# Clustered attention and two gated layers on one core: a new written order of all operations, a third unpack buffer, pair passes in halves

## The chip, the cores and the metric

One core of a Trainium2 chip. The core has five engines that run their own instruction streams at once: TensorE (PE, matrix products and transposes; PEld is its weight load), VectorE (DVE), ScalarE (ACT), GpSimd (POOL), and SyncE (SP), which here issues every DMA. The metric is the device time of one execution in microseconds (us); lower is better.

## The reference

```python
# attention: q, k, v of shape (2, 8, 768, 64), 16 centroids for each of 8 heads
q_assign = argmax(q_n @ c_n.T); k_assign = argmax(k_n @ c_n.T)
mask = q_assign[:, :, :, None] == k_assign[:, :, None, :]
scores = where(mask, q @ k.T / 8, -1e9)
attn = softmax(scores)
x = (attn @ v), heads side by side          # (1536, 512)
# first layer, d_ff 1024
h = (x @ w1) * (x @ w2) @ w3;  x = h @ w_out   # (1536, 512)
# second layer, d_ff 2048
h = x @ w_in;  g = h * clip(h + 3, 0, 6) / 6
out = g @ w_out2                               # (1536, 512)
```

Everything is float32. Accuracy near float32 is kept by splitting an operand into a high and a low part in the `fp32r` format and adding three products (high-high, high-low, low-high).

## The kernel before, in words

The kernel is one flat list of about 4,000 operations (`op(key, engine, ...)`; `fop` is an operation that may run on one of several engines). Two tables written into the file fix everything about the order: `RANK` gives each operation its place in one common list, and `ON` gives a letter (a, d, p for ACT, DVE, POOL) to each operation with a choice. `Plan.order` sorts by `RANK`, and the instructions are emitted in that order. Each engine therefore works through its own operations in list order, and SP issues DMAs in list order; what an operation waits for is its data and a free buffer. `need` and the buffer counts of `Plan({...})` only constrain the list; the durations written beside each operation were for the search that found it.

The work runs in these stages. **Attention**, 16 heads of 768 rows in two halves (`hf`) and six row blocks (`c`): loads `lq`, `lk`, `lv`; transposes `T` on PE, their split `qkh` (ACT) and `qkl` (DVE); `pa`, the products with the centroids; `oh0` to `oh8`, nine small steps that turn them into one-hot codes; the moves `Dk`, `Ek`, `Dq`, `Ck`, `Cq` on SP; the scores `S1` and `S` (L745), the row maximum `mx` (DVE, L757), the exponential `ex` (ACT, L779); the transposes of the probabilities `pT` (L795) and their split into a high part `ph` (ACT) and a low part `pl` (DVE); the products with v, `av` (L819). With `WHOLE = 1`, head 0 alone is not split: its probabilities are copied whole (`p_all`), `pl` does not exist for it, and its `av` runs on plain float32 operands. After each pair of heads, POOL passes finish the pair on 128x768 tiles: `os` (L842, adds the two output parts), `pm` (L877, multiplies by the reciprocal denominators), and for the first four pairs `xh` and `xl` (the split of x for the next layer).

**Weights** are stored so that they have to be unpacked. For each of 72 blocks (`wo`, `w3`, `ab`, `set`): load `ld`, `c0` and `c2` on ACT (into the rings `cvt` and `cvs`), the clamp `c1` (L1002, DVE or POOL), `c3` and `c5` on DVE (L1011, L1015). A `cvs` buffer is free again when its block has been used; for an `ab` block that includes the store `abp` (L1127), which writes the block to DRAM, and for a `set` block the store `sst`. These blocks are interleaved with the attention.

**First layer**: w3 @ w_out is made during attention (`w`, L1062), `ab` (L1138) is x times w1 and w2 of the first four pairs, `x2` (L1253) the product with the combined matrix; the second batch half uses a seven-product scheme (`b`, L1390). **Second layer**: 16 steps `p` of seven products `h` (L1701) and output products `o` (L1745).

`idle` operations are matmuls on the identity whose result is not used; there are six groups of 2 to 5. `root` and `warm` are tiny ACT operations that call Sqrt and Exp; `cen2` (L527) also calls Sqrt.

```python
    def warm(func):
        if "warm" not in W_:
            W_["warm"] = at.tile([128, 1], F32, tag="warm", name="warm")
        nc.scalar.activation(out=W_["warm"], in_=three, func=func)
...
    op("root", "act", 0.2, lambda: warm(AF.Sqrt), due=-60)
    op("warm", "act", 1.4, lambda: warm(AF.Exp), ["cen2"], due=-5, after=[("qkh", 0, 1)])
    op("z", "act", 0.8, lambda: zero_rows(kk_[1]), due=61, after=[("qkh", 0, 1)])
```

Of the kernel before, what the change touches and what calls it, by code (L numbers as in the profile page):

```python
# [1852 lines left out]
```

## Time and profile before

| what | value |
|---|---|
| time, median of 3 runs | 756.61 us (754.64 to 757.69) |
| time of the profiled execution | 753.79 us |
| its span, first to last instruction | 751.9 us |
| first row maximum `mx` of head 0 / head 2 / head 9 / last | 19.8 / 60.4 / 200.7 / 352.5 us |
| first `x2` product in the long run of them, first `h` | 374.6 / 495.8 us |
| PE, DVE, ACT, POOL busy | 727.5, 621.8, 547.7, 196.0 us |

A busy share says how long an engine had an instruction in work, not how full it was: PE's instructions are pipelined. In a list of instructions, what stands in brackets is the idle time of the engine just before the instruction and the engine and tile that ended it. A line such as L426 or L423 is a helper's that many operations share; the tile's name tells which one it is (`cvs<-raw` is `c2`, `cvt<-raw` is `c0`, `pl<-ptr,ph` is `pl`).

### The profile page before, as it was taken

How to read it: one execution, taken by the hardware profiler on the slowest of the kernel's cores; microseconds unless marked ns; L12 is line 12 of the kernel's file. 1: busy time of each engine (PE TensorE's matmuls, PEld its weight loads, DVE VectorE, ACT ScalarE, POOL GpSimd, SP SyncE). 2: the span in 40 equal slices, each digit the busy share in tenths (PEclk: the TensorE clock that was granted, in tenths of full speed). 3: DMA queues.
4: the chain of work that ended last, by engine and by line, in shares of the span. 5: the costliest groups of instructions: out<-in, count | busy, mean ns of one | idle time of the engine just before them, and what ended most of it. 6: DMA issues, size and time to landing. Idle time of an engine off the chain costs nothing.

```text
span 751.9 us, 12041 instructions
## 1 busy us (share of the span) xinstructions
PE 727.5 (97%) x4143; PEld 661.9 (88%) x4143; DVE 621.8 (83%) x1076; ACT 547.7 (73%) x1040; POOL 196.0 (26%) x219
## 2 busy tenths in 40 slices
...
GB/s 217 198 141 174 157 128 201 127 136 125 197 109 159 160 132 178 108 141 86 161 195 224 223 129 112 177 214 128 158 123 70 45 68 130 81 71 80 46 29 85
DMA packets 81741, 101.97 MB, mean 136 GB/s; under 512 B 30960, under 2 KB 56592, under 8 KB 81680
## 3 DMA queue, kind: packets, MB, share of 16 engines
...
## 4 chain that ended last, share of the span: by engine, by line
PE 46%; DVE 4%; ACT 2%; issue 1%; POOL 0%; POOLq 0%; ACTq 0%; DVEq 0%
PE po L1745 16%; PE psh L1701 14%; PE psx L1253 8%; PE psab L1390 7%; PE psab L1138 1%; DVE gh L423 1%; DVE tt L1727 0%; PE av L819 0%; DVE m_gb L1608 0%; ACT tt L1723 0%; DVE m_sn L1715 0%; DVE m_gv L423 0%; ACT m_sn L426 0%; ACT m_whl L426 0%; PE ptr L795 0%
## 5 line engine op out<-in xcount | busy, mean ns | idle before, releaser
L757 DVE TENSOR_REDUCE den<-pst 128x1 f32<-128x768 f32 x96 | 91.2, 950 | 17.3 <-PE pst L745 14.8
L779 ACT ACTIVATE p<-pst,den 128x768 f32<-128x768 f32 x96 | 86.8, 904 | 14.5 <-DVE den L757 13.5
L423 DVE TENSOR_TENSOR pl<-ptr,ph 128x512 fp32r<-128x512 f32 x135 | 89.7, 680 | 7.7 <-ACT ph L426 7.4
L426 ACT ACTIVATE ph<-ptr 128x512 fp32r<-128x512 f32 x135 | 78.4, 596 | 16.1 <-PE ptr L795 14.6
L1138 PE MATMUL psab<-xT,abhl 128*128 128x384 f32 x384 | 81.1, 342 | 5.1 <-ACT asb L426 5.1
L1002 POOL TENSOR_SCALAR cvt<-cvt 128x512 f32<-128x512 f32 x43 | 40.9, 954 | 138.3 <-ACT cvt L426 113.3
L745 PE MATMUL pst<-kk,qkL 128*128 128x512 f32 (+1 forms) x192 | 71.6, 376 | 4.2 <-ACT p L779 3.8
L1138 PEld LDWEIGHTS psab<-xT,abhl 128*128 128x128 f32 x384 | 65.7, 188 | 7.2 <-ACT asb L426 5.8
L795 PEld LDWEIGHTS ptr<-id_r,praw 128*128 128x128 f32 x576 | 60.4, 140 | 7.4 <-ACT p L426 0.8
L819 PE MATMUL av<-ph,vs 128*128 128x384 f32 x180 | 63.3, 352 | 1.8 <-ACT T L426 1.8
L795 PE MATMUL ptr<-id_r,praw 128*128 128x128 f32 x576 | 64.4, 242 | 0.3 <-ACT p L426 0.2
L745 PE MATMUL pst<-kk,qkH 128*128 128x512 f32 (+1 forms) x192 | 64.2, 338 | 0.0
L426 ACT ACTIVATE m_sn<-psh 128x384 f32<-128x384 f32 x64 | 31.2, 488 | 44.2 <-PE psh L1701 43.7
L819 PE MATMUL av<-pl,vs 128*128 128x384 f32 x180 | 61.1, 339 | 0.0
L426 ACT ACTIVATE cvs<-raw 128x512 int32<-128x512 uint8 x72 | 47.9, 669 | 13.1 <-DMA abp<-cvs 7.3
L426 ACT ACTIVATE cvt<-raw 128x512 f32<-128x512 f32 x72 | 48.3, 672 | 11.1 <-DMA raw<-in_moe_w_out_dram 3.4
L1011 DVE SCALAR_TENSOR_TENSOR cvs<-cvt,cvs 128x512 int32<-128x512 int32 x72 | 52.5, 737 | 3.2 <-ACT cvs L426 2.3
L1062 PE MATMUL psw<-woh,wT 128*128 128x512 f32 x128 | 51.1, 414 | 0.0
L1015 DVE SCALAR_TENSOR_TENSOR cvs<-cvt,cvs 128x512 int32<-128x512 int32 x72 | 50.1, 699 | 0.3
L745 PEld LDWEIGHTS pst<-kk,qkL 128*128 128x128 f32 x192 | 36.0, 187 | 15.6 <-ACT p L779 12.6
L1723 ACT ACTIVATE tt<-m_sn,three 128x384 f32<-128x384 f32 x48 | 29.4, 613 | 19.5 <-DVE m_sn L1715 8.1
L1745 PE MATMUL po<-m_hl,m_gv 128*128 128x512 f32 x144 | 40.4, 393 | 0.0
...
## 6 DMA issues: line engine op xcount, KB each, us to landing
...
```

The lines of the kernel that those rows point to most:

```text
L423: nc.vector.tensor_tensor(out=out, in0=a, in1=b, op=ALU.subtract)
L426: nc.scalar.activation(out=out, in_=in_, func=AF.Copy, **kw)
L745: x = mm(out=psr[:, t, ks_], lhsT=TT[nm, h][:, i, cs_], rhs=flat(TT["K", h][:, a])[:, ks_], start=st, stop=sp)
L757: done["mx", n] = [other_banks(nc.vector.tensor_reduce(out=den_at(h, 0, c), in_=psS[h, c], axis=AX.X, op=ALU.max, negate=True), ("S", n + 1))]
L779: done["ex", n] = [other_banks(nc.scalar.activation(out=p, in_=psS.pop((h, c)), func=AF.Exp, bias=den_at(h, 0, c), accum_out=den_at(h, 1, ...
L795: x = nc.tensor.transpose(pt[:, blk(j)], raw[h, hf][0][:, c, blk(kb)], id_r)
L819: mm(out=t[:, 0:HF], lhsT=vs_t[h][:, 2 * s + i, :], rhs=x_[:, c0:c0 + HF], start=(s == 0 and i == 0 and n == 0), stop=(s == 2 and i == 1 a ...
L1138: mm(out=ps[:, 0:HF], lhsT=s[:, w, a, blk(kk)], rhs=xT0[0][:, x_, kk, hf * HF:hf * HF + HF], start=(kk == 0 and n == 0), stop=(kk == KD - ...
L1253: mm(out=ps[:, 0:HF], lhsT=Whl[0][:, a, j, blk(d)], rhs=gh[:, g_, j, :], start=(j == 0 and n == 0), stop=(j == J1 - 1 and n == 2))
L1390: mm(out=ps[:, 0:HF], lhsT=t[:, l, a, blk(kk)], rhs=bx[r][:, x_, kk, :], start=(st and kk == 0 and m == 0), stop=(kk == 1 and m == 2), ski ...
L1701: mm(out=ps[:, 0:HF], lhsT=left(p, l, a, kk), rhs=x[:, x_, kk, :], start=(st and kk == 0 and m == 0), stop=(kk == 1 and m == 2), skip_grou ...
L1745: mm(out=outs[b, c], lhsT=g[:, a, blk(c % 3)], rhs=w[:, w_, :], start=(first and a == 0 and w_ == 0), stop=(last and a == 1))
```

## The change

All of `RANK` is replaced, and twelve strings of `ON`. Beside the order, the code changes in five places: the ring `cvs` has three buffers in place of two; `os`, `pm` and `xl` are issued twice, on the 384 columns of each half, so that 19 POOL passes become 38, and `ab` products of a half need the `xl` of that half alone; `WHOLE` goes from 1 to 0, so head 0 is split as all others are; `cen2` may not come ahead of `root`; the first `ex` of a head may not come ahead of `warm`.

The two `RANK` tables can be compared between marks of the list. Operations of an engine that differ in number, before and after:

| list from / to | DVE | ACT | POOL |
|---|---|---|---|
| start / `S1` of head 0 | `c3` 2, 3; `oh0` 1, 2; `wtl` 1, 0; `Ck` 2, 1; `c1` 2, 1 | `root`, `warm`, `z`, `Ck` 0, 1 each; `c2` 2, 3; `wth` 2, 1 | `vlo` 1, 0; `oh1` 0, 1; `c1` 1, 2 |
| `S1` of head 0 / of head 2 | `pl` 3, 12; `wtl` 2, 3; `c3` 7, 6; `c1` 3, 2; `oh0` 2, 1; `oh1` 1, 0; `oh4` 1, 0 | `root` 1, 0; `z` 1, 0; `c0` and `c2` 7, 6; `ph` 12, 13 | `vlo` 1, 3; `vhi` 1, 2; `oh4` 1, 2 |
| `S1` of head 2 / of head 9 | `c1` 2, 4; `c3` 17, 16; `woh` 2, 1; `oh1` 1, 0; `oh4` 0, 1; `pw` 4, 5 | | `c1` 15, 13 |
| last `S` / first `x2` | `Wl` 1, 2; `pl` 6, 9; `c5` 2, 3; `c1` 1, 0 | | `Wl` 3, 2; `c1` 1, 2 |
| first `x2` / first `h` | `c1` 10, 18; `c3` 20, 23; `c5` 21, 23; `xwl` 6, 7; `Ll` 3, 4; `wol2` 3, 2 | `c0` 22, 24; `c2` 21, 23 | `c1` 10, 6 |

At the start, the DVE list before runs, from head 0's `oh0`: `oh0` to `oh4`, `c5`, `oh5`, `oh6`, `qkl` of head 1, `oh8`, another `qkl`, two `Ck`, `wtl`, `oh0` of head 1, `mx`. After: `oh0` to `oh4`, `qkl` of head 1, `oh5`, `oh6`, `c3`, `oh0` of head 1, `oh8`, one `Ck`, `c3`, `c5`, `c5`, `mx`; one `qkl` of head 1 stands ahead of `oh0`, and on PE half of head 1's transposes ahead of head 0's `pa`. The `idle` groups ahead of the first `S1` hold 11 matmuls before and 6 after; the first of them goes from place 5 to place 40.

```diff
@@ RANK
-    "root": "186",
-    "warm": "449",
-    "z": "105",
-    "idle": "5 79 97 112 45 37",
+    "root": "3",
+    "warm": "51",
+    "z": "43",
+    "idle": "40 62 135 151 81 100",
...
@@ ON
-    "Ck": "dd",
+    "Ck": "ad",
-    "pw": "pppdppppddapdpppaaapadddpdddddpp",
+    "pw": "ppppddppaaadaddpaaappappddapdpdd",
-    "oh1": "pddppppppddppdp",
+    "oh1": "pppppppppdpddpp",
-    "oh4": "pdppppppppdpppd",
+    "oh4": "ppdpppppppppppp",
-    "xh": "paaa",
+    "xh": "aaaa",
-    "woh": "adppddpp",
+    "woh": "appdaapd",
-    "Wl": "dppp",
+    "Wl": "pddp",
-    "Ll": "dddpdddpdddddddddddddddddpdddddd",
+    "Ll": "dddddddddddddddppddddddddddddddd",
-    "wol2": "ddddddddddddpdpdppdpppddpdpdddpd",
+    "wol2": "ddpddddddppdddddddddppddddddpdpp",
-    "xwl": "pddddddpdddddp",
+    "xwl": "dddddddddddddd",
-    "xs": "dddddddd",
+    "xs": "ddddddpd",
-    "c1": "ppddpdppddpdppppppppppppppdpdpppddpddpdpppppppdpdddpddppdppppppddddddddd",
+    "c1": "pppppdppdpdpdpppppddpppppdppdpdppppdppdpddddppddddppddppddddppddpdpdpddd",
...
-        "raw": 2, "rawx": 6, "cvt": 2, "cvs": 2, "hl": 2, "wT": 3, "m": 1, "s": 3, "r": 2, "a": 1, "x": 1, "x1b": 1,
+        "raw": 2, "rawx": 6, "cvt": 2, "cvs": 3, "hl": 2, "wT": 3, "m": 1, "s": 3, "r": 2, "a": 1, "x": 1, "x1b": 1,
...
-    op("cen2", "act", 0.2, cen_2, ("cen1",), due=-13.9)
+    op("cen2", "act", 0.2, cen_2, ("cen1", "root"), due=-13.9)
...
-    PHL, P32, WHOLE = [], [], 1
+    PHL, P32, WHOLE = [], [], 0
...
-    def o_sum(pr):
-        nc.gpsimd.tensor_tensor(out=Ts[pr], in0=Ts[pr], in1=W_["o"], op=ALU.add)
+    def o_sum(pr, hf):
+        nc.gpsimd.tensor_tensor(out=Ts[pr][:, hf], in0=Ts[pr][:, hf], in1=W_["o"][:, hf], op=ALU.add)
...
-    def pair_mul(pr):
-        T, rd = flat(Ts[pr]), flat(rdb.pop(pr))
-        if pr == KD:
+    def pair_mul(pr, hf):
+        r = slice(HF * hf, HF * hf + HF)
+        T, rd = flat(Ts[pr])[:, r], flat(rdb[pr])[:, r]
+        if pr == KD and hf == 0:
             xT1[0] = base.tile([128, KD, S], F32, tag="x1b", name="xT1")
-        out = T if pr < KD else xT1[0][:, pr - KD, :]
+        out = T if pr < KD else xT1[0][:, pr - KD, r]
         nc.gpsimd.tensor_tensor(out=out, in0=T, in1=rd, op=ALU.mult)
...
-    def pair_lo(e, pr):
-        sub_on(e, xT0[0][:, 1, pr, :], flat(Ts.pop(pr)), xT0[0][:, 0, pr, :])
+    def pair_lo(e, pr, hf):
+        r = slice(HF * hf, HF * hf + HF)
+        sub_on(e, xT0[0][:, 1, pr, r], flat(Ts[pr])[:, r], xT0[0][:, 0, pr, r])
...
-            op(("ex", h, c), "act", 0.88, lambda c=c: sexp(h, c), [("mx", h, c)] + [("ex", h, c - 1)] * (c > 0), due=t + 0.6, take=("p",),
+            op(("ex", h, c), "act", 0.88, lambda c=c: sexp(h, c), [("mx", h, c)] + ([("ex", h, c - 1)] if c else ["warm"]), due=t + 0.6, take=("p",),
...
-            nd = [("dB", h - 1), ("dB", h), ("oa", h, 0), ("oa", h, 1), ("oa", h - 1, 0), ("oa", h - 1, 1)]
             x = pr < KD
-            if oap(h):
-                op(("os", pr), "pool", 1.8, lambda: o_sum(pr), nd[2:], due=e + 3, drop=("O",))
-                nd = nd[:2] + [("os", pr)]
-            op(("pm", pr), "pool", 1.8, lambda: pair_mul(pr), nd, due=e + 4, drop=("rdb",) if x else ("rdb", "T"),
-               take=("x1b",) if pr == KD else ())
+            for hf in range(2):
+                nd = [("oa", h, hf), ("oa", h - 1, hf)]
+                if oap(h):
+                    op(("os", pr, hf), "pool", 0.93, lambda hf=hf: o_sum(pr, hf), nd + [("os", pr, 0)] * hf, due=e + 3 + 0.1 * hf, drop=("O",) * hf)
+                    nd = [("os", pr, hf)]
+                nd += [("dB", h - 1), ("dB", h)] + [("pm", pr, 0)] * hf + [("pm", KD, 0)] * (pr > KD)
+                op(("pm", pr, hf), "pool", 0.93, lambda hf=hf: pair_mul(pr, hf), nd, due=e + 4 + 0.1 * hf,
+                   drop=(("rdb",) if x else ("rdb", "T")) if hf else (), take=("x1b",) if pr == KD and hf == 0 else ())
             if x:
-                fop("xh", ("xh", pr), {"a": 0.75, "p": 0.9, "d": 0.5}, lambda e: pair_hi(e, pr), [("pm",
-                    pr)] + [("xh", 0)] * (pr > 0), due=e + 4.5, take=("x",) if pr == 0 else ())
-                fop("xl", ("xl", pr), {"p": 1.8, "d": 0.87}, lambda e: pair_lo(e, pr), (("xh", pr),), due=e + 4.6,
-                    drop=("T",))
+                fop("xh", ("xh", pr), {"a": 0.75, "p": 0.9, "d": 0.5}, lambda e: pair_hi(e, pr), [("pm", pr, 0), ("pm", pr, 1)]
+                    + [("xh", 0)] * (pr > 0), due=e + 4.5, take=("x",) if pr == 0 else ())
+                for hf in range(2):
+                    fop("xl", ("xl", pr, hf), {"p": 0.93, "d": 0.47}, lambda e, hf=hf: pair_lo(e, pr, hf),
+                        [("xh", pr)] + [("xl", pr, 0)] * hf, due=e + 4.6 + 0.1 * hf, drop=("T",) * hf)
...
-            s = cvo[key] = base.tile([128, 512], I32, tag="cvs", name="cvs", bufs=2)
+            s = cvo[key] = base.tile([128, 512], I32, tag="cvs", name="cvs", bufs=3)
...
-                       [("abl", j, w), ("xl", kk)] + ([("ab", j, hf, w, kk - 1)] if kk else []),
+                       [("abl", j, w), ("xl", kk, hf)] + ([("ab", j, hf, w, kk - 1)] if kk else []),
...
-        t = W_["osb", b, c] = base.tile([128, DM], F32, tag=("cvt", "cvs")[c % 2], name="osb", bufs=2)
+        t = W_["osb", b, c] = base.tile([128, DM], F32, tag=("cvt", "cvs")[c % 2], name="osb", bufs=(2, 3)[c % 2])
```

## Rows read from the trace of the kernel before

**Rows 1.** The profile's page: busy time, share of the span, instructions.

```profile
PE 727.5 (97%) x4143; PEld 661.9 (88%) x4143; DVE 621.8 (83%) x1076; ACT 547.7 (73%) x1040; POOL 196.0 (26%) x219
```

**Rows 2.** Windows: start:end, length, busy us of PE PEld DVE ACT POOL, granted clock.

```profile
0.00:19.80 19.80, 12.70 (x48) 9.59 (x49) 15.91 (x42) 9.81 (x17) 4.19 (x28) 1.00 0.79 217
19.80:60.40 40.60, 36.23 (x192) 26.81 (x191) 33.87 (x56) 37.06 (x69) 13.26 (x20) 1.00 0.59 159
104.40:142.50 38.10, 38.10 (x238) 32.70 (x237) 37.45 (x67) 34.58 (x70) 19.78 (x24) 1.00 0.55 146
352.50:374.60 22.10, 21.89 (x136) 20.81 (x133) 17.32 (x28) 18.11 (x31) 11.85 (x7) 1.00 0.40 135
374.60:495.80 121.20, 120.97 (x696) 120.65 (x697) 113.67 (x196) 80.45 (x142) 20.49 (x12) 1.00 0.55 179
```

**Rows 3.** Timeline, three stretches: ACT and PE.

```profile
209.03 0.66 ACT L426 ACTIVATE cvs<-raw 128x512 int32<-128x512 uint8 x1 [2.87 <-DMA abp<-cvs]
...
210.12 0.79 PE L1138 MATMUL psab<-xT,abhl 128*128 128x384 f32 x3 [2.85 <-ACT asb L426]
...
227.73 0.66 ACT L426 ACTIVATE cvs<-raw 128x512 int32<-128x512 uint8 x1 [1.83 <-DMA abp<-cvs]
...
229.45 0.44 PE L819 MATMUL av<-ph,vs 128*128 128x384 f32 x1 [1.63 <-ACT T L426]
...
301.17 0.66 ACT L426 ACTIVATE cvs<-raw 128x512 int32<-128x512 uint8 x1 [2.61 <-DMA abp<-cvs]
...
302.75 1.84 PE L1138 MATMUL psab<-xT,abhl 128*128 128x384 f32 x9 [2.11 <-ACT asb L426]
```

**Rows 4.** Timeline, 39.9 to 47 us: start, length, operation, idle before it.

```profile
39.95 1.28 ACT L505 ACT_TABLE_LOAD   x1
...
41.25 0.20 ACT L505 ACTIVATE warm<-three 128x1 f32<-128x1 f32 x1
...
43.51 1.28 ACT L779 ACT_TABLE_LOAD   x1
...
46.46 0.96 DVE L757 TENSOR_REDUCE den<-pst 128x1 f32<-128x768 f32 x1 [2.40 <-PE pst L745]
```

**Rows 5.** Timeline, transposes of head 1.

```profile
13.47 1.17 PE L607 MATMUL ptqk<-id_f,qkn 128*128 128x128 f32 x6
```

**Rows 6.** Groups by line: busy us, mean ns, idle before. Whole span.

```profile
L423 DVE TENSOR_TENSOR pl<-ptr,ph 128x512 fp32r<-128x512 f32 x135 | 89.7, 680 | 7.7 <-ACT ph L426 7.4
...
L420 POOL TENSOR_TENSOR vs<-vn,vs 128x384 fp32r<-128x384 f32 x15 | 15.3, 1018 | 0.6
...
L842 POOL TENSOR_TENSOR T<-T,O 128x768 f32<-128x768 f32 x7 | 13.4, 1915 | 12.9 <-ACT T L426 12.7 <-DMA qkH<-cd 0.2
...
L660 DVE STREAM_TRANSPOSE as<-pa 128x384 f32<-128x384 f32 x16 | 9.1, 569 | 0.1
...
L662 DVE TENSOR_TENSOR as<-as 128x192 f32<-128x192 f32 x6 | 2.7, 444 | 0.1
...
L668 DVE TENSOR_TENSOR as<-as,wtab 128x192 f32<-128x192 f32 x4 | 1.4, 358 | 0.1
```

**Rows 7.** Timeline around 38 us, POOL and DVE.

```profile
37.91 1.27 POOL L420 TENSOR_TENSOR wol<-cvs,woh 128x512 fp32r<-128x512 f32 x1
38.03 1.44 DVE L1002 TENSOR_SCALAR cvt<-cvt 128x512 f32<-128x512 f32 x1
```

**Rows 8.** The DMA stores of L1127 (abp).

```profile
DMA to landing us min/median/max: 2.0/2.7/4.1
```

**Rows 9.** Groups by line, DVE, 374.6 to 495.8 us.

```profile
L1015 DVE SCALAR_TENSOR_TENSOR cvs<-cvt,cvs 128x512 int32<-128x512 int32 x20 | 14.0, 700 | 0.1
...
L1011 DVE SCALAR_TENSOR_TENSOR cvs<-cvt,cvs 128x512 int32<-128x512 int32 x20 | 13.4, 685 | 0.6 <-POOL cvt L1002 0.5
...
L1002 DVE TENSOR_SCALAR cvt<-cvt 128x512 f32<-128x512 f32 x10 | 4.2, 418 | 0.0
...
L423 DVE TENSOR_TENSOR b_x<-xT,b_x 128x768 fp32r<-128x768 f32 x3 | 2.8, 947 | 0.0
```

More of the change, by code (lines that the diff above doesn't have):

```diff
@@ L61 @@
     "qkl": """
-        27 29 54 59 161 164 283 285 437 434 562 573 701 706 824 818 941 939 1056 1058 1184 1189 1307 1310 1453 1450 1576 1580 1700
-        1715 1860 1866""",
[3 rows of a table removed]
+        23 26 37 50 170 194 291 295 448 442 578 582 708 712 829 835 953 949 1082 1081 1199 1209 1331 1328 1459 1457 1591 1610 1736
+        1744 1871 1883""",
[3 rows of a table added]
     "Ck": """
-        67 62 139 136 253 249 370 383 532 525 646 659 786 795 903 898 1033 1035 1163 1155 1289 1271 1403 1408 1540 1536 1679 1673 1831
-        1823 1966 1950""",
+        70 69 155 140 269 252 417 405 542 548 671 668 795 791 923 929 1053 1048 1169 1178 1295 1291 1398 1411 1554 1556 1712 1702 1829
+        1833 1965 1969""",
@@ L106 @@
+        1967 2019 2073 2119""",
     "pT": """
[5 rows of a table removed]
-        2070 2086 2102 2114 2115 2134 2135""",
-    "ph": """
[5 rows of a table removed]
-        2073 2103 2108 2120 2124 2142 2144""",
[5 rows of a table added]
+        2101 2106 2122 2132 2144 2151 2171""",
+    "ph": """
[5 rows of a table added]
+        2111 2127 2133 2142 2155 2172 2174""",
+    "pl": """
[5 rows of a table added]
+        2116 2139 2143 2163 2167 2175 2177""",
     "av": """
[3 rows of a table removed]
-        1947 1980 1998 2017 2030 2049 2058 2089 2092 2118 2138 2149 2153""",
[3 rows of a table added]
+        1996 2028 2030 2048 2060 2089 2093 2117 2125 2147 2168 2178 2183""",
@@ new lines @@
+        2477 2770 2814 2680 3060 2492 2906 2978 3171 2721 2276 3108 2529 3190 2603 2802 2852""",
[5 rows of a table added]
+    "w": """
+        115 169 191 226 247 258 266 277 290 294 318 325 340 356 363 367 386 399 419 424 443 450 463 468 496 504 525 539 554 596 633
+        642 664 672 691 705 750 754 769 790 812 823 827 830 888 892 928 933 959 968 988 1009 1040 1045 1051 1080 1110 1127 1136 1151
+        1175 1180 1186 1191""",
[6 rows of a table added]
+    "ab": """
[5 rows of a table added]
+        2205 2209 2212""",
+    "aba": "1255 1330 1471 1412 1549 1599 1705 1767 1831 1882 1978 2021 1951 2169 2086 2200",
@@ L214 @@
+    "abg": "1283 1380 1502 1530 1646 1679 1733 1796 1854 1922 2001 2061 2146 2192 2123 2236",
+    "xdone": "2214",
+    "Wh": "2103 2120 2136 2158",
+    "Wl": "2110 2128 2149 2166",
+    "top": "2201",
+    "gsh": "2206 2210 2213 2219 2223 2234 2254 2295",
+    "gsl": "2211 2217 2221 2227 2231 2251 2279 2306",
+    "x2": """
[5 rows of a table added]
+        2911 2913 2915""",
[6 rows of a table added]
     "bsm": """
-        2225 2231 2290 2296 2316 2335 2364 2366 2381 2390 2396 2409 2420 2423 2426 2428 2461 2479 2490 2509 2531 2532 2535 2560 2568
@@ L236 @@
+    "bs": """
+        2347 2363 2369 2376 2408 2424 2434 2440 2463 2478 2484 2489 2521 2531 2538 2544 2574 2589 2597 2602 2620 2636 2641 2646 2665
+        2676 2682 2688 2704 2716 2722 2731""",
[8 rows of a table added]
     "sst": """
-        2491 2397 2297 2111 2121 2243 2328 2342 2236 2391 2200 2685 2595 2451 2162 2458 2794 2908 2842 3154 2635 3015 2836 3208 2747
-        2286 2954 2515 3211 2753 3056 3067""",
+        2546 2428 2302 2152 2097 2259 2358 2381 2247 2438 2207 2686 2559 2425 2185 2482 2831 2817 2684 3079 2496 2910 3029 3215 2725
+        2280 3113 2533 3225 2608 2805 2896""",
@@ L244 @@
-        3222 3223 3229 3289 3291 3292 3294 3340 3342 3344 3345 3392 3423 3432 3434 3495 3501 3502 3506 3565 3569 3586 3590 3633 3636
-        3639 3642 3703 3706 3708 3717 3766 3767 3770 3782 3835 3837 3838 3846""",
+        2819 2833 2843 2850 2892 2895 2898 2901 2951 2958 2965 2976 3024 3031 3035 3041 3106 3111 3114 3117 3160 3162 3164 3165 3248
+        3252 3255 3256 3298 3306 3310 3313 3367 3374 3380 3390 3439 3445 3454 3456 3506 3508 3510 3511 3561 3564 3566 3582 3643 3650
+        3657 3662 3710 3713 3727 3728 3785 3788 3789 3791 3845 3870 3871 3880""",
@@ L251 @@
-        3663 3730 3740 3795 3812 3871 3890""",
+        2861 2868 2909 2916 2985 2991 3049 3062 3127 3139 3199 3207 3265 3273 3325 3337 3397 3408 3462 3472 3530 3540 3601 3606 3681
+        3686 3745 3761 3800 3806 3896 3906""",
     "wf": """
-        2742 2752 2767 2840 2869 2914 2933 3054 3039 3167 3113 3220 3184 3264 3288 3382 3322 3418 3430 3474 3523 3522 3585 3637 3634
-        3746 3702 3775 3749 3796 3868 3870""",
+        2808 2838 2835 2894 2888 3026 3002 3104 3070 3184 3181 3249 3221 3311 3348 3414 3420 3478 3498 3520 3531 3614 3617 3676 3694
@@ L255 @@
+        3712 3738 3768 3838 3851 3909 3907""",
     "woh2": """
-        2757 2785 2801 2887 2902 3001 3007 3132 3074 3206 3163 3255 3263 3359 3311 3411 3381 3446 3476 3514 3577 3621 3602 3670 3697
-        3771 3731 3789 3791 3842 3927 3921""",
+        2822 2866 2878 2930 2928 3057 3030 3131 3175 3237 3209 3279 3272 3342 3388 3437 3465 3503 3512 3547 3585 3668 3640 3703 3718
+        3755 3777 3841 3852 3865 3927 3935""",
     "wol2": """
-        2763 2828 2863 2897 2926 3049 3020 3157 3093 3210 3177 3258 3283 3366 3314 3414 3426 3455 3493 3518 3581 3626 3631 3694 3699
@@ L282 @@
     "hr": """
[L283 to L285 removed]
+        2938 2952 2963 2966 2989 3010 3019 3022 3066 3080 3088 3094 3134 3151 3170 3172 3201 3228 3236 3244 3275 3293 3304 3309 3360
```

148 lines of the change are left out of this document (64 added, 84 removed), and 243 rows, old and new, of the table RANK.

## The prediction

> **What bounds the kernel now.** I read the page first. TensorE is busy 97% of the span, VectorE 83%, ScalarE 73%, GpSimd 26% [rows 1]. So nothing that shortens another engine's work counts unless TensorE was waiting for it, and there are only 751.9 - 727.5 = 24.4 us of such waiting. The table by stretch tells where it lies [rows 2]. The start (0 to 19.8 us) has PE idle for 7.1 us, the first two heads (19.8 to 60.4) for 4.4 us. From 104.4 to 142.5 PE is busy throughout, but so is VectorE, at 37.45 of 38.1 us, 98.3%: in the attention VectorE is close behind, and 98.3% is the fullest that I see it run. From 374.6 to 495.8, PE idles 0.2 us and VectorE 7.5 of 121.2 us. The granted clock is 1.00 in each stretch shown.
>
> The instructions in order of time then show where PE waits in the middle. Three times ScalarE's `c2` waits for the store `abp` that still reads the `cvs` buffer it wants: 2.87, 1.83 and 2.61 us, in all 7.3 us. Behind `c2` on ScalarE stand the copies that PE waits for (`asb`, or `T` from `av`), and PE stands idle 2.85, 1.63 and 2.11 us right after, in all 6.6 us [rows 3]. A second place is a pair of table loads: `root` loads Sqrt's table at 39.95 and `ex` loads Exp's again at 43.51, each 1.28 us on ScalarE; at 46.46 VectorE has stood 2.40 us waiting for scores [rows 4].
>
> **The change part by part.** The sum is made against the profiled execution's 753.8 us, which is 2.8 us below the median of 756.6; the same difference is then taken from the median.
>
> *Start.* Half of head 1's transposes come ahead of head 0's `pa`; that is half of an operation pair, and one of them took 1.17 us [rows 5]. On VectorE, between `oh0` and the first `mx`, one more `c3` and `c5` and `oh0` of head 1 (ahead of `oh8`) come in; one `Ck`, the `wtl` and one `qkl` leave. The chain pa, oh0 to oh8, Ck, S1, mx sets this stretch's end. If all that is put in falls into waits, it costs 0; if the transposes (1.17) and head 1's `oh0` (0.57, [rows 6]) lie on the chain, with a little of the unpacking, it costs 2. I take +1.0.
>
> *First two heads, 19.8 to 60.4.* Head 0 is now split. VectorE gets 9 more `pl`, and `wtl`, a subtraction of the same size (10 x 0.680 = 6.8), and loses `oh0`, `oh1`, `oh4` (0.569 + 0.444 + 0.358 = 1.4) [rows 6], one `c3` and one clamp (0.685 + 0.418 = 1.1, [rows 9]): +4.3, so 33.87 + 4.3 = 38.2 us. PE gets the split products in place of the plain float32 ones, which I count at nothing, because PE had 4.4 us to spare there [rows 2]. ScalarE is rid of both loads, 2.56 us [rows 4], and gets one `ph`. The two waits that come in (`cen2` for `root`, the first `ex` for `warm`) cost nothing: on ScalarE, which would hold up all that is queued behind them, both awaited operations stand earlier in its own order. So VectorE sets this stretch: at its fullest share, 38.2 / 0.983 = 38.8 us against 40.6, or -1.8. The bounds: all of the 2.40 us wait gone (-2.4); or VectorE fills no more of its time here than before (33.87 / 40.6 = 83%): the 4.3 less the 2.56 of the loads stay, +1.7.
>
> The Trainium skill, page "ScalarE: Activation LUTs", section "What ACT_TABLE_LOAD costs", counts a drain of some 1.38 us beside the load of 1.28. Here `warm` begins 0.02 us after its load's end [rows 4], so no drain shows behind the load; with it, the estimate by that page would free 5.3 us of ScalarE in place of 2.6, and the stretch would still be set by VectorE.
>
> *Port gaps.* A clamp on VectorE took 1.44 us under a GpSimd subtraction of 1.27 us [rows 7]; alone it takes 0.42 [rows 9], so one clash costs 1.0 us of VectorE. It matters only where VectorE sets the pace, that is from 60 to 200 us. I take 0.8 us there (below: nothing; above: 1.7, the price of a clash and two thirds of another). The halved passes stand beside this: a 128x384 subtraction took 1.018 us on GpSimd, and a 128x768 addition 1.915 [rows 6], so a pair of halves costs 0.1 us more than the whole, 2 us for 19 of them. GpSimd is idle three quarters of the span, which hides it, and without that cover 2 us is the cost; a half comes ready 0.9 us earlier.
>
> *Third `cvs` buffer.* The stores land 2.0 to 4.1 us after issue, 2.7 at the median [rows 8]. With a third buffer a `c2` takes a buffer whose store lies one block further back. I laid both lists out with the durations of the trace: for several `ab` blocks only 0.7 to 3.0 us of VectorE work lay between the store and the `c2` that takes its buffer before; afterwards it is 4.7 or more everywhere, which is beyond 4.1. So the 6.6 us of PE idle go. The other bound is 0. What the stall hid would be late next: `cvt` keeps two buffers, and `c0` stands in front of `c2`. I take -6.6, the value of [rows 3].
>
> *After the attention, 374.6 to 495.8.* Here the list brings VectorE 8 clamps that GpSimd did (8 x 0.418), 3 `c3` (0.685), 2 `c5` (0.700) and, net, one subtraction (`xwl` and `Ll` in, a `wol2` out; 0.947): 3.3 + 2.1 + 1.4 + 0.9 = +7.7 [rows 9]. That makes 113.67 + 7.7 = 121.4 us, as much as the whole stretch lasts. At 98.3% it lasts 123.5, so +2.3. If all of it fell into VectorE's 7.5 us of waits it would cost 0.2; if those waits stay, +7.7.
>
> The sum: +1.0 - 1.8 - 0.8 - 6.6 + 2.3 = -5.9. The profiled time becomes 747.9, the median 756.6 - 5.9 = **750.7 us**. What I have not named (heads 2 to 15, the second layer) is bound by PE with the same products and counts as zero.
>
> **The rivals.** What can be told from no change is 0.5%, 3.8 us: below 752.8 or above 760.4.
>
> *The wait moves on.* The third buffer frees ScalarE from waiting for the store, but `c2` then stands on data or on `cvt`, or the new order has its own late copy. For it: `cvt` and the raw buffers are as they were. Against: in the trace, each of the three stalls is put down to the store. Half of the 6.6 lost gives 754.0, all of it 757.3.
>
> *VectorE becomes the bound after the attention.* The 7.5 us that it idles from 374.6 to 495.8 are waits for PE's results that cannot be filled, so all of +7.7 stays; and from 352.5 to 374.6, where it has 4.8 us idle [rows 2], the list adds a `Wl` (two `pl`, 1.4), three `pl` (2.0) and a `c5` (0.7) less a clamp, 3.7. That gives 750.7 + 5.4 + 3.7 = 759.8, slower than before. It decides the sign once more than 5.9 us of these 9.1 are paid. For it: 98.3% was reached in one stretch only, and this one is the third as long as all attention. Against: VectorE has no long wait in it now.
>
> *PE's clock stays at its lower level (1.2 GHz) for part of the first two heads.* Before the first `S1` 6 unused products stand where 11 stood, and the first group comes at place 40 of the list, not 5. The column has 1.00 in the first 19.8 us [rows 2], with PE busy 64% of them, after those products. If a quarter of the next stretch's 36.2 us of PE work ran at half speed, 9.1 us more less the 4.4 idle give +4.7, 755.4; for half of it, +13.7, 764.4. It is slower than before by more than 0.5% from two fifths on. Against: the split products of head 0 give PE more work there. The Trainium skill, page "TensorE: Matmul & The Clock Gate", Part 1 on the clock gate, has the low level as the default and activity as what lifts it; no row here shows the low level.
>
> **How the numbers follow.** The forecast gets 0.60; the moved wait 0.20; VectorE late 0.13; the clock 0.07. The forecast's own range: everything at its better bound is -1.0 (start), -0.6, -0.9, -2.1, so 746.1; the worse bounds are not likely together, and the two largest (first heads +3.5, late +5.4, of which half each) give 755.2. For 8 in 10 over all cases I go a little below the better bound, for a gain that I did not find, and up to VectorE's case: 744.5 to 760.0. Faster by over 0.5%: 0.55 of the forecast's 0.60 and 0.03 of the moved wait, 0.58. Slower by over 0.5%: 0.09 from the VectorE case, with a bad start beside it, and 0.05 from the clock, 0.14. The rest, 0.28, is the same.
>
> **What the profile would show.** Right: no `cvs<-raw` with idle time put down to `abp`, and no PE idle of over 1.5 us behind an ACT `asb` or `T`; two table loads fewer; the first `mx` near 20.8 us, that of head 2 some 0.8 us earlier than now; the `x2`-to-`h` stretch near 123.5 us with VectorE at 98%. Wrong: a new wait of ScalarE on `cvt` or on raw data in the middle; VectorE below 94% and a longer stretch after 374.6; granted clock under 1.00 before 60 us. What would make the prediction wrong beyond that is an order that makes PE idle at many small places, which a sum of named terms cannot see.

## The result, and the profile after

The changed kernel took **747.21 us** at the median (746.43 to 748.33), against 756.15 us for the kernel before (754.64 to 757.69) in the same comparison: ratio 0.9883, 95% interval 0.9858 to 0.9907, 8.9 us less. The forecast was 750.7, in a range of 744.5 to 760.0; faster was right, and the size was forecast a third too small. The profiled execution took 746.43 us, its span 744.5. One execution among the experiments below, of e5, ran at a granted clock of 0.853 (787.66 us); it is left out of its ratio.

The page of the changed kernel, busy time of each engine (answers to [rows 1]):

```profile
PE 721.8 (97%) x4143; PEld 660.8 (89%) x4143; DVE 619.3 (83%) x1086; ACT 548.7 (74%) x1046; POOL 175.6 (24%) x229
```

The windows of the changed kernel between the same marks of the work: start, first `mx` of head 0, of head 2, of head 8, of head 14, first product of the long run of `x2`, first `h`, end. Columns as in [rows 2]; the last two are the DMA share and GB/s.

```profile
0.00:21.40 21.40, 9.46 (x39) 7.99 (x40) 14.96 (x41) 12.53 (x21) 5.33 (x29) 1.00 0.84 237
21.40:58.40 37.00, 34.32 (x210) 28.56 (x209) 36.14 (x63) 33.05 (x67) 17.24 (x24) 1.00 0.71 171
58.40:177.70 119.30, 118.47 (x748) 103.31 (x747) 115.46 (x201) 109.71 (x221) 51.16 (x67) 1.00 0.56 153
177.70:303.20 125.50, 125.14 (x823) 117.86 (x822) 113.86 (x193) 107.50 (x221) 54.03 (x67) 1.00 0.55 152
303.20:360.00 56.80, 56.22 (x362) 53.26 (x361) 46.75 (x77) 45.00 (x86) 24.28 (x23) 1.00 0.46 143
360.00:488.70 128.70, 126.92 (x723) 124.59 (x722) 124.04 (x216) 89.32 (x156) 6.47 (x8) 1.00 0.59 189
488.70:744.40 255.70, 251.23 (x1249) 225.27 (x1247) 168.08 (x304) 151.55 (x278) 17.07 (x12) 1.00 0.25 82
```

And the kernel before between the same marks, for the stretches that [rows 2] does not have:

```profile
60.40:180.30 119.90, 119.47 (x762) 104.48 (x761) 116.60 (x202) 107.52 (x217) 53.90 (x67) 1.00 0.56 151
180.30:314.10 133.80, 126.69 (x825) 118.72 (x824) 115.56 (x199) 107.84 (x219) 50.50 (x54) 1.00 0.58 155
314.10:369.70 55.60, 55.34 (x357) 52.33 (x356) 43.93 (x75) 44.52 (x85) 25.39 (x21) 1.00 0.40 120
369.70:495.70 126.00, 125.66 (x722) 124.66 (x721) 118.47 (x202) 85.25 (x150) 21.42 (x13) 1.00 0.55 177
```

(The long run of `x2` begins at 369.7 us there; the 374.6 of the small table and of [rows 2] lies 5 us inside it. The stretch is taken from its begin here.)

The reader sees where the 7.4 us between the two spans come from: start +1.6, heads 0 and 1 -3.6, heads 2 to 7 -0.6, **heads 8 to 13 -8.3**, last heads to `x2` +1.2, `x2` to `h` +2.7, the rest -0.4. In heads 8 to 13 PE stood idle 133.80 - 126.69 = 7.1 us before and 0.4 after; the other 1.6 us of the 8.3 are busy time of PE (126.69 to 125.14 us), and in the two stretches behind PE is busy 2.1 us longer than before. Outside heads 8 to 13 the whole new order comes out at +0.9.

The groups by line of the changed kernel show that the wait on the store is gone (the first line is the kernel before), that `cvt` waits no longer than the 11.1 us of before, and that the clamps on GpSimd have a mean of 700 ns (954 before):

```profile
L426 ACT ACTIVATE cvs<-raw 128x512 int32<-128x512 uint8 x72 | 47.9, 669 | 13.1 <-DMA abp<-cvs 7.3 <-DMA set<-cvs 5.7
...
L427 ACT ACTIVATE cvt<-raw 128x512 f32<-128x512 f32 x72 | 48.2, 671 | 9.1 <-DVE cvs L1021 4.6 <-DMA raw<-in_moe_w_in_dram 1.9 <-DMA raw<-in_moe_w_dram 1.7
L427 ACT ACTIVATE cvs<-raw 128x512 int32<-128x512 uint8 x72 | 48.1, 668 | 0.0
...
L1008 POOL TENSOR_SCALAR cvt<-cvt 128x512 f32<-128x512 f32 x40 | 27.9, 700 | 149.1 <-ACT cvt L427 125.4 <-DVE b_sn L1405 21.4 <-ACT praw L769 0.9
```

`c2` now waits for nothing, 0.0 us in 72, although the `abp` stores land later than before (median 4.8 us and at most 5.0 from issue to landing, against 2.7 and 4.1 in [rows 8]).

### The profile page after: what moved, and what is told of

It is laid out like the page before. It is cut to its first block, busy times and chain, and to the rows that moved or that the text cites. A ratio compares the mean times of both kernels' runs of the same rounds, so it can differ in the third digit from the quotient of the medians.

```text
span 744.5 us, 12074 instructions
## 1 busy us (share of the span) xinstructions
PE 721.8 (97%) x4143; PEld 660.8 (89%) x4143; DVE 619.3 (83%) x1086; ACT 548.7 (74%) x1046; POOL 175.6 (24%) x229
## 4 chain that ended last, share of the span: by engine, by line
PE 79%; DVE 9%; ACT 5%; DMA 4%; issue 2%; SPq 1%; POOL 0%; ACTq 0%; DVEq 0%; POOLq 0%
PE po L1751 17%; PE psh L1707 15%; PE pst L746 8%; PE av L820 8%; PE psab L1396 7%; PE psab L1144 7%; PE ptr L796 5%; PE psw L1068 5%; PE psx L1259 4%; DMA m_gb<-set 2%; PE pa L647 1%; DVE den L758 1%; ACT p L780 1%; PE ptqk L608 1%; DVE cvs L1017 1%
## 5 line engine op out<-in xcount | busy, mean ns | idle before, releaser
L424 DVE TENSOR_TENSOR pl<-ptr,ph 128x512 fp32r<-128x512 f32 x144 | 95.4, 679 | 6.8 <-ACT ph L427 6.1
L427 ACT ACTIVATE ph<-ptr 128x512 fp32r<-128x512 f32 x144 | 83.0, 594 | 10.5 <-PE ptr L796 8.2
L820 PE MATMUL av<-ph,vs 128*128 128x384 f32 x192 | 67.5, 352 | 0.0
L820 PE MATMUL av<-pl,vs 128*128 128x384 f32 x192 | 64.9, 338 | 0.3 <-DVE pl L424 0.3
L1008 POOL TENSOR_SCALAR cvt<-cvt 128x512 f32<-128x512 f32 x40 | 27.9, 700 | 149.1 <-ACT cvt L427 125.4
L427 ACT ACTIVATE m_sn<-psh 128x384 f32<-128x384 f32 x64 | 31.3, 489 | 32.0 <-PE psh L1707 31.3
L1017 DVE SCALAR_TENSOR_TENSOR cvs<-cvt,cvs 128x512 int32<-128x512 int32 x72 | 50.3, 702 | 1.4 <-issue 0.6
L1021 DVE SCALAR_TENSOR_TENSOR cvs<-cvt,cvs 128x512 int32<-128x512 int32 x72 | 49.5, 692 | 0.6
L1751 PE MATMUL po<-m_whl,m_gv 128*128 128x512 f32 x171 | 45.8, 392 | 0.0
```

The source lines that it names most:

```text
L424: nc.vector.tensor_tensor(out=out, in0=a, in1=b, op=ALU.subtract)
L427: nc.scalar.activation(out=out, in_=in_, func=AF.Copy, **kw)
L820: mm(out=t[:, 0:HF], lhsT=vs_t[h][:, 2 * s + i, :], rhs=x_[:, c0:c0 + HF], start=(s == 0 and i == 0 and n == 0), stop=(s == 2 and i == 1 a ...
L1017: stt(out=s, in0=cvt[key], scalar=3, in1=s, op0=ALU.logical_shift_left, op1=ALU.bitwise_or)
L1751: mm(out=outs[b, c], lhsT=g[:, a, blk(c % 3)], rhs=w[:, w_, :], start=(first and a == 0 and w_ == 0), stop=(last and a == 1))
```

## The experiments

In the edits, `MOVE` gives operations another place in the common list (35.3 is just behind place 35) and `ENG` another engine; all else stays. Every ratio is to the kernel before, on the same chip: e1 to e4, e5 to e8, e9 to e11 and e12 ran on four chips, and the median of before was 756.3, 756.8, 756.7 and 754.6 us there. Where two runs come from different chips, their ratios are the measure and the medians stand beside them.

| run | kernel | median us | ratio, 95% interval |
|---|---|---|---|
| e1 | before, `cvs` 3 | 747.78 | 0.9887 (0.9865 to 0.9908) |
| e2 | before, two table loads fewer | 753.58 | 0.9959 (0.9943 to 0.9975) |
| e3 | before, head 0 split | 759.80 | 1.0045 (1.0031 to 1.0060) |
| e4 | before, e1 + e2 + e3 | 749.03 | 0.9903 (0.9884 to 0.9923) |
| e5 | before, e1 + e2 | 744.81 | 0.9841 (0.9817 to 0.9865) |
| e6 | changed, head 0 unsplit | 749.89 | 0.9912 (0.9890 to 0.9934) |
| e7 | changed, transposes of head 1 put back | 747.47 | 0.9879 (0.9860 to 0.9899) |
| e8 | changed, 8 late clamps on GpSimd | 745.54 | 0.9854 (0.9833 to 0.9875) |
| e9 | e7, and the copies `cT` put back | 746.71 | 0.9869 (0.9849 to 0.9889) |
| e10 | e4, `pl` of head 0 later, 5 operations to GpSimd | 748.01 | 0.9897 (0.9876 to 0.9918) |
| e11 | changed, `os` and `pm` whole | 747.28 | 0.9878 (0.9859 to 0.9898) |
| e12 | e8 + e9, and PE's product `cT` put back | 744.26 | 0.9857 (0.9834 to 0.9879) |

**e1: the third buffer alone.**

```diff
-        "raw": 2, "rawx": 6, "cvt": 2, "cvs": 2, "hl": 2,
+        "raw": 2, "rawx": 6, "cvt": 2, "cvs": 3, "hl": 2,
...
-            s = cvo[key] = base.tile([128, 512], I32, tag="cvs", name="cvs", bufs=2)
+            s = cvo[key] = base.tile([128, 512], I32, tag="cvs", name="cvs", bufs=3)
...
```

> The kernel before, with a third cvs buffer and nothing else; its order is unchanged. Theory 1 (the store's wait is a matter of buffers): the three waits of ScalarE's cvs<-raw on the store (7.3 us) are gone, PE's 6.6 us of idle time behind them too, and the time falls by 6 to 7 us, ratio 0.991 to 0.992. Rival (the wait moves on): ScalarE reaches c2 earlier, but the old order lets it stand on cvt or on raw data instead; PE keeps half or more of the idle time, and the ratio is 0.996 to 1.000.

It gave 8.5 us, practically all that the whole change gave, in the order of before. The groups of ScalarE in e1:

```profile
L426 ACT ACTIVATE cvt<-raw 128x512 f32<-128x512 f32 x72 | 48.4, 672 | 14.1 <-DMA raw<-in_moe_w_in_dram 5.1 <-DMA raw<-in_moe_w_out_dram 3.5 <-DMA raw<-in_moe_w_dram 2.0
L426 ACT ACTIVATE cvs<-raw 128x512 int32<-128x512 uint8 x72 | 48.0, 671 | 0.1
```

`cvs` waits 0.1 us in place of 13.1, of which 5.7 were for the stores `set<-cvs` behind the attention; the stretches there are no shorter in e1 (from `x2` to `h` 126.5 us against 126.0, the rest 257.0 against 256.2). `cvt` waits 3 us longer over the span (11.1 before), but not where PE pays. Heads 8 to 13 in e1:

```profile
181.00:308.70 127.70, 126.63 (x827) 118.77 (x826) 116.76 (x200) 107.48 (x219) 50.47 (x54) 1.00 0.62 163
```

127.7 us against 133.8: 6.1 us, close to the 6.6 of [rows 3]. That the median fell by 2 us more is taken up with e2. The profiled execution of e1 is the slowest of its five: its granted clock fell at the first scores of head 0 (0.84 and 0.73), where no store is waited for, and the first `mx` of head 2 comes at 61.0 us against 60.4:

```profile
16.00:20.00 4.00, 2.75 (x12) 2.07 (x13) 3.89 (x8) 2.50 (x5) 1.84 (x4) 0.84 0.81 242
20.00:24.00 4.00, 3.63 (x15) 2.45 (x15) 3.84 (x8) 3.78 (x7) 1.61 (x3) 0.73 1.01 270
```

**e2: two table loads fewer.**

```diff
+MOVE = {"root": 2.5, "warm": 49.5}
```

> The kernel before, with root ahead of cen2 and warm ahead of head 0's first exponential, so that two of four table loads go (2.57 us of ScalarE). Theory 1 (the loads hold up the scores at 40 to 46 us): the first mx of head 2 comes 1 to 2.4 us earlier and the time falls by as much, ratio 0.997 to 0.999. Rival (VectorE or PE holds this stretch anyway): head 2 comes less than 0.5 us earlier, ratio 1.000.

The first `mx` of head 2 came at 57.8 in place of 60.4 (2.4 us of it in the stretch behind the first `mx`), and the median fell by 2.7 us: the first theory. But in e2's profiled execution the lead of 3.0 us at head 9 was 0.2 at head 10. The wait on the store lies there, and the windows and the instructions in order of time of e2 show what followed it:

```profile
200.00:204.00 4.00, 4.00 (x30) 3.80 (x30) 3.55 (x7) 3.14 (x7) 1.76 (x2) 1.00 1.02 260
204.00:208.00 4.00, 0.80 (x6) 0.66 (x5) 1.67 (x5) 1.62 (x4) 1.10 (x3) 0.78 0.12 46
208.00:212.00 4.00, 4.00 (x14) 3.81 (x13) 1.23 (x2) 2.00 (x5) 0.00 (x0) 0.50 0.42 131
212.00:216.00 4.00, 4.00 (x27) 3.77 (x27) 3.68 (x6) 2.26 (x5) 0.68 (x2) 0.86 0.04 8
216.00:220.00 4.00, 4.00 (x29) 3.83 (x29) 2.97 (x4) 3.50 (x8) 2.06 (x2) 1.00 0.75 182
```

```profile
206.38 0.66 ACT L432 ACTIVATE cvs<-raw 128x512 int32<-128x512 uint8 x1 [3.19 <-DMA abp<-cvs]
207.47 1.33 PE L1144 MATMUL psab<-xT,abhl 128*128 128x384 f32 x3 [3.20 <-ACT asb L432]
```

PE stood idle 3.20 us, and then had a granted clock of 0.50, its lower level of 1.2 GHz, from 208 to 212: 14 matmuls in 4 us where 29 and 30 ran in 4 us at 1.00. From the first `mx` of head 9 to that of head 10 e2 needs 25.3 us, the profiled execution of before 22.5, where the same wait (2.85 us, [rows 3]) was followed by a clock of 1.00. First e2, then before:

```profile
197.70:223.00 25.30, 22.10 (x130) 20.66 (x129) 17.90 (x31) 17.64 (x38) 8.03 (x9) 0.87 0.48 124
200.70:223.20 22.50, 19.64 (x129) 18.24 (x128) 17.87 (x32) 17.64 (x38) 8.01 (x9) 1.00 0.53 137
```

For the same products PE was busy 22.10 us in place of 19.64. So a store's wait costs its own length, and in e2 it cost 2.5 us more in clock. In e3, which has two buffers too, the clock fell behind another of the three waits, one of 2.15 us, and not behind those of 2.03 and 2.08:

```profile
308.00:312.00 4.00, 4.00 (x16) 4.00 (x15) 2.06 (x5) 2.07 (x4) 0.81 (x1) 0.57 0.65 211
```

PE's three waits together are much the same in each of these executions: 6.6 us before, 7.2 in e2, 6.3 in e3. Over the 48 executions of the kernel before that these comparisons timed, the mean granted clock lies between 0.993 and 1.000, and the time goes with it (correlation -0.81): the 15 at 0.995 have a median of 757.5 us, the 5 at 1.000 one of 754.6. The profiled execution of before was one at 1.000 (753.8). With the third buffer it is 1.000 in four of e1's five. The means over the 48 and the five, 0.9970 and 0.9994, make an estimate of 0.24% of 754 us, 1.8 us, which is about what the median of e1 gained beyond the 6.6. That the clock makes up all of it is not shown: at 1.000 alone, e1's four have a median of 747.2 and the five of before, on other chips, 754.6, still 7.4 us apart. Nor does a third buffer keep the clock up everywhere: the changed kernel's four executions lie between 0.997 and 1.000, and e4's six go down to 0.995.

**e3, e4, e5: head 0 split in the old order, and the parts together.** e3 puts each `pl` of head 0 right behind its `ph`; e4 and e5 take parts together.

```diff
-    PHL, P32, WHOLE = [], [], 1
+    PHL, P32, WHOLE = [], [], 0
```

> The kernel before, with head 0 split as the other heads (each pl of head 0 right behind its ph). By the prediction's pricing (VectorE sets the first two heads, PE's saving is worth nothing): VectorE has 6.1 us more there, the first mx of head 2 comes 2 to 5 us later. Rival (PE sets them; head 0's products take 8.2 us of PE in float32 and 4.2 us split): the first mx of head 2 comes up to 4 us earlier, ratio 0.995 to 0.999.

> The kernel before with the three parts of e1 to e3 at once, in the order of before. Theory 1 (the parts are worth what they are worth in any order): ratio near the product of the three, and if that is 0.987 to 0.990 the new order itself adds nothing beside the parts. Rival (the order is worth something of its own): the three together stay 2 us or more above the changed kernel, ratio 0.991 or more.

> The kernel before with the third cvs buffer (e1) and two table loads fewer (e2), head 0 unsplit, order otherwise as before. If the gains add up: 756.3 - 8.5 - 2.7 = 745.1, ratio 0.985, and it beats the changed kernel by 1 to 2 us without any of the new order. Rival (e2's gain was won from the waits that e1 removes, or is lost again): 747 to 748, ratio 0.988 to 0.989.

In the old order the split costs 3.5 us (e3), and 0.0062 in ratio, 4.7 us, without the store's waits (e4 against e5). The stretch of heads 0 and 1 says the same: 44.2 us in e3 against 40.6, and 42.5 in e4 against 38.2 in e2. The buffer and the two loads add up: 744.8 us against the 745.1 worked out, with nothing of the new order. (No profile of e5 is read here.) e4 lies between its two theories; e5 decides: the changed kernel is no faster than two of its parts in the old order (2.4 us slower at the median; the intervals overlap a little, 0.9858 to 0.9907 and 0.9817 to 0.9865), so on balance its order shows no worth of its own beside them. The stretch of heads 0 and 1 in e4:

```profile
20.60:63.10 42.50, 34.19 (x192) 26.56 (x191) 37.85 (x64) 33.78 (x65) 13.62 (x20) 1.00 0.56 151
```

PE has 34.2 us of work, as in the changed kernel, but stands idle 8.3 us. Its waits there, by line (`pst` holds the scores, `p` the exponentials, `ptr` the transposed probabilities):

```profile
PE pst L752 <- ACT p L786: 4.0, 6, 1.3
PE ptr L802 <- DVE pl L430: 2.4, 4, 1.3
```

**e6: head 0 unsplit in the new order.**

> The changed kernel with head 0 left unsplit, as it was before (its nine pl gone from the list, all else in place). If the split pays in the new order (PE sets the first two heads): the first mx of head 2 comes 1 to 4 us later, ratio to before 0.990 to 0.994. Rival (VectorE sets them, as e3 has it for the old order, where splitting cost 3.5 us): it comes 1 to 3 us earlier, ratio 0.984 to 0.987.

Here the split pays: without it the kernel is 2 to 3 us slower (0.0029 in ratio, with intervals that overlap), and the stretch of heads 0 and 1, which decides it, is 40.0 us in place of 37.0:

```profile
21.90:61.90 40.00, 37.30 (x210) 29.12 (x209) 31.33 (x53) 33.00 (x67) 16.64 (x24) 1.00 0.68 158
```

PE is busy 37.3 in place of 34.3 us, VectorE 31.3 in place of 36.1. The new order runs VectorE at 36.14 / 37.00 = 97.7% there, and PE's shorter work comes through: the stretch is 3.0 us shorter, PE is busy 3.0 us less and idle 2.7 us in both. But unsplit, the new order needs 40.0 us where the old one with the same table loads needs 38.2 (e2). Of the 3.6 us that the change gains in this stretch, the loads make 2.4; the new order costs 1.8 and its split gives 3.0 back.

**e10: is it VectorE's load?** e4, with each `pl` of head 0 half of the way towards the place where its buffer is wanted again, and three clamps and two one-hot steps moved to GpSimd.

> The kernel of e5 (order of before, third buffer, two loads fewer) with head 0 split, but unlike e4 each pl of head 0 stands later behind its ph, as far as three PSUM buffers let it, half of the way, and five other operations of VectorE in this stretch (three clamps, oh1 and oh4 of head 2; 2.1 us) go to GpSimd. If VectorE's load is what makes the split cost (e4 against e5: 4.2 us): 745 to 747, ratio 0.985 to 0.988, so half or more of that cost is gone. If PE's saving of 4 us shows once VectorE has room, as it does in the new order: 741 to 743, ratio 0.979 to 0.982. Rival (the place of pl does not matter): 748 to 749, ratio 0.990.

748.0 us, ratio 0.9897 against 0.9903 of e4: neither theory of load is borne out, and the rival holds.

```profile
21.30:62.50 41.20, 33.59 (x192) 26.60 (x191) 36.28 (x59) 33.62 (x65) 16.89 (x25) 1.00 0.58 155
```

VectorE has the 36 us that it has in the changed kernel, in 41.2 us in place of 37.0, and PE still waited 3.7 us for `p` and 3.2 for `pl`; in the changed kernel it waits 2.5 there for `p` and not for `pl`. So load does not tell why the split fits the new order and not the old; that leaves the place of the other operations, which no run tested.

**e7, e9, e12: the start.** e7 puts head 1's transposes back behind `pa`; e9 also VectorE's two copies `cT`; e12 also PE's product for them, and takes e8's clamps along.

```diff
+MOVE = {("T", 1, 0): 35.3, ("qkh", 1, 0): 36.5, ("qkl", 1, 0): 39.5}    # e7
+        ("cTc", 0): 22.3, ("cTc", 1): 22.4,                              # e9, besides
+        ("cT", 0): 16.5,                                                 # e12, besides
```

> The changed kernel with the first transposes of head 1 and the copy and subtraction behind them put back behind head 0's pa, as before. In the changed kernel these transposes wait 1.33 us for the load of k and hold up pa. If that sets the start: pa and the first mx come 1 to 1.5 us earlier and the time falls by as much, ratio to before 0.986 to 0.987. Rival (PE's way to the first scores has another bound, such as the wait for c3 on VectorE): mx moves by under 0.5 us, ratio 0.988.

> The kernel of e7 (head 1's first transposes behind head 0's pa), and also VectorE's two copies cT put back ahead of the first qkl, as before. In e7 pa did not come earlier: it began 0.14 us after those copies' end, at 11.90. If the copies set pa: pa begins near 11.0, the first mx comes 0.8 to 1.5 us earlier than e7's 21.9, ratio to before 0.985 to 0.987. Rival (the way from oh8 over the copies Ck and Cq, split between two engines, sets mx, and what is won ahead of it is lost there): mx moves by under 0.5 us, ratio 0.988.

> The changed kernel with e8's eight clamps on GpSimd and the start of e9, in which also PE's product cT (tile pc) stands ahead of head 0's transposes again, as before. In the changed kernel and in e9 this product waits behind the transposes for the load of k, and pa waits for it through VectorE's copies. If that sets the start: pa begins near 10.8 us, the first mx near 20.3, 1.0 to 1.5 us earlier than the changed kernel; with e8's 1.7 us the time is 744 to 745, ratio 0.982 to 0.985, as good as e5. Rival (what is won ahead of the first mx is lost behind it, or the start has yet another bound): mx after 21 us, or the same time as e8, ratio 0.985 to 0.986.

e7 and e9 missed: their first `mx` comes at 21.9, and the four profiles with the changed kernel's start (the changed kernel, e6, e8, e11) have it from 21.4 to 21.9. PE in order of time, first in the changed kernel:

```profile
8.43 1.51 PE L608 MATMUL ptqk<-id_f,qkn 128*128 128x128 f32 x6 [8.43 <-DMA qkn<-in_k_dram]
9.59 0.56 PE L556 MATMUL pc<-id_r,cs 128*128 128x128 f32 x2
11.48 0.87 PE L608 MATMUL ptqk<-id_f,qkn 128*128 128x128 f32 x3 [1.33 <-DMA qkn<-in_k_dram]
12.12 0.66 PE L647 MATMUL pa<-qkH,cT 128*128 128x384 f32 x1
```

and in e12:

```profile
6.89 0.49 PE L562 MATMUL pc<-id_r,cs 128*128 128x128 f32 x2 [6.89 <-DVE id_r L507]
8.66 1.51 PE L614 MATMUL ptqk<-id_f,qkn 128*128 128x128 f32 x6 [1.28 <-DMA qkn<-in_k_dram]
10.25 0.66 PE L653 MATMUL pa<-qkH,cT 128*128 128x384 f32 x1
```

The product `pc` needs only the centroids, but in the new list it stands on PE behind transposes that wait for the load of k; through VectorE's copies `pa` waits for it. Put ahead, `pa` begins at 10.25 in place of 12.12 and the first `mx` comes at 20.6 in place of 21.4. Of the 1.9 us that `pa` gains, 1.5 are left at `oh0` (13.77 to 12.23), 0.4 at `oh1` (14.39 to 14.02) and 0.75 at `oh8` (18.49 to 17.74). What takes most of it back is a `qkl` of head 1, which stands behind `oh0` in e12's list and waits for ScalarE:

```profile
13.48 0.62 DVE L624 SCALAR_TENSOR_TENSOR qkL<-ptqk,qks,qkH 128x384 fp32r<-128x384 f32 x1 [0.67 <-ACT qkH L621]
```

So the gain at `mx` is less than the 1.0 to 1.5 us expected. Whether it reaches the end of the kernel the times do not show: e12's ratio (0.9857) is no better than that of e8 alone (0.9854), as the rival had it, and its median of 744.3 us comes from a chip on which the kernel before is 2 us faster too.

**e8: the late clamps.**

```diff
+ENG = {("c1", "set", 4, 0): "pool", ("c1", "set", 1, 0): "pool", ...}    # 8 of the 18
```

> The changed kernel with 8 of the 18 clamps that VectorE does between the first x2 and the first h given back to GpSimd, which is idle there (6.5 of 128.7 us). If VectorE's 124.0 us of work set that stretch: it gets 3.3 us shorter work, the stretch shrinks by 1 to 2 us, ratio 0.985 to 0.987. Rival (clamps on GpSimd stretch VectorE's own instructions by as much as they free, or PE sets the stretch): no gain, ratio 0.988.

1.7 us less at the median, 0.0029 in ratio; the intervals of e8 and of the changed kernel overlap, but the stretch itself shows it:

```profile
360.40:487.70 127.30, 126.01 (x722) 124.68 (x721) 122.09 (x208) 89.00 (x156) 18.68 (x15) 1.00 0.59 190
```

127.3 in place of 128.7 us, with VectorE 2.0 us less busy: on VectorE these clamps cost the stretch 1.4 us. e12 repeats the gain: from `x2` to `h` 486.5 - 359.2 = 127.3 us again. The other profiles leave little room for chance: this stretch is 126.0 to 126.5 us in the six of the old order and 128.5 to 128.7 in the five of the new order without e8's clamps.

**e11: the halves undone.**

```diff
-        nc.gpsimd.tensor_tensor(out=Ts[pr][:, hf], in0=Ts[pr][:, hf], in1=W_["o"][:, hf], op=ALU.add)
+        if hf:
+            nc.gpsimd.tensor_tensor(out=Ts[pr], in0=Ts[pr], in1=W_["o"], op=ALU.add)
...
```

`pm` is changed in the same way; `xl` stays in halves.

> The changed kernel with os and pm issued once for both halves, at the place of the second half (xl stays in halves). By the prediction (GpSimd is idle three quarters of the time and hides them): no change, ratio to before 0.987 to 0.989, within 1 us of the changed kernel. Rival (the halves free the tile T, or give x to PE, in time): PE waits for x, 1 to 3 us more, ratio 0.990 to 0.992.

No difference: 747.28 against 747.21 us, ratio 0.9878 against 0.9883. GpSimd hides the passes `os` and `pm` whole or halved. The profiled execution has a lower clock in head 0, behind a wait of PE of 1.76 us between the first scores; the first `mx` of head 2 comes at 58.7 all the same (58.4 in the changed kernel, whose clock was 1.00 there):

```profile
20.00:24.00 4.00, 3.66 (x11) 2.89 (x12) 4.00 (x8) 3.63 (x8) 1.00 (x2) 0.58 1.09 256
```

e5 and e12 are 0.0042 and 0.0026 in ratio below the changed kernel (2.4 and 3.0 us at the median); which of the two is better their intervals don't tell, and they were not combined.

## Why the prediction was right, point by point

The sum was -5.9 us, the profiled executions differ by 7.4, the medians by 8.9.

- **The third buffer (-6.6): right in mechanism, undersized.** The wait went and PE's idle time with it (heads 8 to 13: -6.1 in e1; -8.3 with the change, of which 6.7 idle time). e1 measured the whole at 8.5 us at the median. What the term left out is the clock behind the wait, which the profiled execution of before happened not to show (1.00 in all rows) and those of e2 and e3 did; that it makes up the 2 us is an estimate. The reason given, a margin of 4.7 us of VectorE's work against stores that land within 4.1, did not hold as it stood: the stores of the changed kernel took up to 5.0 us. That `c2` waits for none of them is measured; how much room was left is not. The Trainium skill, page "TensorE: Matmul & The Clock Gate", Part 1 on the clock gate, was cited for a rival in the first heads, with activity as what lifts the clock; the traces show a lower clock in both places, in the first heads (0.73 in e1, 0.58 in e11) and behind the store's wait (0.50 in e2, 0.57 in e3).
- **First two heads (-1.8): -3.6.** The step that failed is "PE gets the split products ..., which I count at nothing". PE's saving, 3.0 us of busy time, came through, as e6 shows, while the new order runs VectorE at 97.7%. VectorE's own sum was too high (38.2 reckoned, 36.1 measured). With 36.1 the prediction's rule gives 36.1 / 0.983 = 36.8 us, close to the 37.0, but the rule is not borne out: without the split VectorE has 4.8 us less to do and the stretch is 3.0 us longer (e6). The two loads were worth 2.4 us in this stretch and 2.7 at the median (e2), at the top of the bounds. The old order could not have taken the split (e3, e4), so the sign of this term hung on the order, which a count of work cannot see. The term came out beyond its better bound of -2.4; what it left out, 1.8 us that the order costs and 3.0 that the split gains, partly cancelled, and that was luck.
- **Start (+1.0): +1.6, for another reason.** The transposes put ahead were not the cause by themselves (e7); the centroids' product moved behind them was, at least in part (with both put back, e12 has the first `mx` 0.8 us earlier than the changed kernel, and 1.3 earlier than e9). I had not looked at where `cT` went.
- **Port gaps (-0.8): -0.6** for heads 2 to 7, which is hardly clear of the spread (119.7 to 120.0 us in the six profiles of the old order, 119.0 to 120.6 in the seven of the new). No run tested the cause.
- **After the attention (+2.3): +2.7**, VectorE at 124.0 of 128.7 us, 96% and not the 98.3% reckoned; e8 shows that the clamps moved there are paid for, with 1.4 us. At 98.3%, VectorE's 124.0 us would need 126.2, so its load does not explain all of the 2.7. PE itself is busy 1.3 us longer there (125.66 to 126.92); what makes up the rest stays open. From 314 us to `x2` +1.2, which the sum left out and the second rival had.
- **The halves (0): 0** (e11; for `os` and `pm`).
- **The rivals.** The wait did not move on: `cvt` waits 9.1 us (11.1 before) in the changed kernel, and in e1, where it waits 14.1, PE does not wait for it. VectorE's late load cost something, but at most 2.7 + 1.2 = 3.9 us of the 9.1 that this rival could cost. The clock was 1.00 through the first two heads in the changed kernel's profile; in e1's and e11's it was not, and cost at most 0.7 us there. The argument against this rival was wrong: the split gives PE less busy time there, not more (34.3 us against 37.3 in e6).
